# An XCiT attention and FFN kernel on one core: two transposes put together, loads reordered, one product for a whole and a left tile

## The chip, the cores and the metric

One core of a Trainium2 chip runs the whole kernel. The metric is the device time of one execution in microseconds (us). Executions are compared by their medians and by a ratio with a 95% interval.

## The reference

```python
def _attn_ref(q, k, v, tau):                      # q, k, v: 4 x 5824 x 256, fp32
    qn = q / (norm(q, axis=1) + 1e-06)            # norms run over the 5824 tokens
    kn = k / (norm(k, axis=1) + 1e-06)
    s = kn.transpose(0, 2, 1) @ qn / tau          # 256 x 256 scores for each batch
    a = np.exp(s - s.max(-1, keepdims=True))
    a /= a.sum(-1, keepdims=True) + 1e-09
    return v @ a

def _moe_ref(x, w1, w2, w3, w_out):               # x: 23296 x 256; w1, w2: 256 x 1024
    h = (x @ w1) * (x @ w2) @ w3                  # w3: 1024 x 1024
    return h @ w_out                              # w_out: 1024 x 256; out: 23296 x 256, fp32
```
(`norm` is written short for numpy's norm with its axis kept.)

## The kernel before

The kernel never forms `v @ a`. For each batch it folds the softmax matrix into w1 and w2 (eight "folds" into `Wf`), and it folds w3 and w_out into one matrix `W_sb` (eight "W units", once). What is left for each token is: two projections a and b of the transposed v by `Wf`, the product a*b, and one product with `W_sb`. A batch has eleven chunks of 512 tokens and a last chunk of 192: a "whole" tile of 128 tokens and 64 "left" ones. The left tokens of two batches are put together into one tile of 128, which is multiplied in the odd batch.

A step j of a chunk is four matmuls into PSUM banks of the tag "ab" (four banks), an ACT copy of a, a DVE product, and, two steps later (`LAG = 2`), the out matmuls into banks of the tag "out" (three banks):

```python
def emit_ab(b, c, j):
    ...                                    # 2 x 2 matmuls into tiles[0], tiles[1], tag "ab"
    nc.scalar.copy(a_sb[:, :n], tiles[0][:, :n])
    ...
    if n == 4 * P:
        nc.vector.tensor_mul(ab, a_sb, tiles[1])
    else:                                  # the 192-token chunk
        nc.vector.tensor_mul(ab[:, :P], a_sb[:, :P], tiles[1][:, :P])
        ...
        nc.vector.tensor_mul(lefts[b // 2][:, j, b % 2, :], a_sb[:, P:n], tiles[1][:, P:n])

def emit_out(b, c, j, ab):
    ...
    if small:
        lhs = [ab[:, :P]]
        if b % 2 == 1:
            lhs.append(lefts[b // 2][:, j, :, :].rearrange("p b t -> p (b t)"))
    ...
    for s, lhsT in enumerate(lhs):         # whole tile first, then the left tile
        ...
        nc.tensor.matmul(tl[h][:, o, :], lhsT=lhsT, rhs=W_sb[:, j, :], ...)
```

The sums of the softmax and the W units:

```python
def sum_mm(c2):
    ...
    if c2 == CT - 1:
        nc.vector.tensor_scalar_add(rs, m[:, :CT], 1e-9)
        nc.vector.reciprocal(rs, rs)

def w_unit(jt):
    m = psum.tile([P, 512], F32, tag="ab", name=f"w_{jt}", bufs=4)
    for lt in range(FT):
        nc.tensor.matmul(m[:, :D], lhsT=w3T[jt // 2][:, jt % 2, lt, :], rhs=wout_sb[:, lt, :], ...)
```

Everything else is put in order by an agenda: a list of works with the time, on a modelled clock, at which each is put into the program. While the chunks of a batch run, the agenda loads the pieces of v, q and k for later (through POOL's queue), transposes v by DMA, and in between computes scores, norms, exponentials and folds of the next batch. The load that follows a v piece is kept back by a "hold", a tiny POOL copy that reads what the transpose of that piece wrote, so that POOL's queue stands until the transpose is done.

```python
moves = [("qk", 1, 0, 29.0), ("v", 0, 3, 30.0), ("qk", 1, 1, 43.0), ("qk", 1, 2, 47.0), ("v", 0, 4, 53.0)]
moves += [("qk", 1, 3, 62.0), ("qk", 1, 4, 66.0), ("v", 0, 5, 72.0), ("qk", 1, 5, 81.0)]
moves += [("v", 1, 0, 94.0), ("v", 1, 1, 104.0), ("v", 1, 2, 114.0), ("qk", 2, 0, 126.0)]
t0, t1 = 54.0, 113.0
...
    if before is not None:
        at(t, 0.0, lambda w=before: hold(...))
...
soft = soft_units(n)                       # norms, k row, q norm, scores, exponentials, sums, folds
for i, (cst, t, fn) in enumerate(soft):
    at(t1 + 1.0 + t + (2.0 if b == 0 and i > 0 else 0.0), cst, fn)
```

## Time and profile before

| | before |
|---|---|
| device time, median of 3 runs | 572.44 us (572.33 to 573.01) |
| span of the profiled execution | 570.48 us |
| first projection starts | 37.59 us |
| first W unit starts, last W matmul starts | 64.61, 75.20 us |
| last matmul starts | 566.54 us |

How to read what follows. In a timeline a line gives the start in us, the length in us, the engine, the line of the kernel, the operation, what it writes and reads, and in brackets how long the engine had stood idle and what released it. In the table of waits a line gives the waiting instruction, what released it, the total us, the number of times and the longest. In the groups the columns are: busy us and mean ns of one, then the idle time before them.

TensorE's waits in the kernel before (the end of the table, without those for the first loads):

```profile
PE sum L328 <- ACT e L318: 0.8, 1, 0.8
PE a L463 <- DVE Wf L387: 0.6, 1, 0.6
PE w L627 <- ACT as L469: 0.2, 1, 0.2
PE a L463 <- ACT as L469: 0.2, 1, 0.2
PE fold L350 <- ACT as L469: 0.2, 1, 0.2
PE b L463 <- ACT Wf L357: 0.2, 1, 0.2
```

Each occurs once and none is over 0.8 us. The last three all fall between 168 and 182 us, where batch 0 goes over into batch 1.

The groups of DVE that the change touches (split by shape):

```profile
L480 DVE TENSOR_TENSOR abs<-as,b 128x128 bf16<-128x128 bf16 x32 | 9.1, 285 | 5.1 <-ACT as L469 2.9 <-PE o L504 0.7
L483 DVE TENSOR_TENSOR left<-as,b 128x64 bf16<-128x64 bf16 x32 | 6.9, 215 | 0.0
...
L334 DVE TENSOR_SCALAR rs<-sum 128x2 f32<-128x2 f32 x4 | 0.6, 153 | 0.4 <-PE sum L328 0.4
```

The two products of the 192-token chunks are 32 pairs; one addition of 1e-9 for each batch.

### The profile page before, as it was taken

To read this page: it belongs to the slowest core of one execution; us is meant where nothing else is said; L and a number is where in the kernel's file an instruction comes from. 1 tells how busy PE (TensorE), PEld (TensorE's weight loads), DVE (VectorE), ACT (ScalarE), POOL (GpSimd) and SP (SyncE) were. 2 spreads that over 40 slices of the span, in tenths; PEclk is the share of its full clock that TensorE was granted. 3 is DMA by queue.
4 is the path that set the end of the run, shared out by engine and by line. 5 is a ranking of instruction groups with operands and counts; after the bars stand their busy time and mean duration, and the time that the engine had idled before them with its cause. 6 is when DMAs were issued, how large, how long until landed. Compare 5 with 4: busy or idle time off the path is not lost.

```text
span 570.5 us, 10131 instructions
## 1 busy us (share of the span) xinstructions
PE 558.5 (98%) x3753; PEld 354.8 (62%) x3753; DVE 377.7 (66%) x613; ACT 339.9 (60%) x627; POOL 77.5 (14%) x164
## 2 busy tenths in 40 slices
PE   7889999999999999999999999999999999999997
PEld 4764576776656666666666666666665666666565
DVE  1047645788967577888766667787867656565564
ACT  1047535777765577777665567777766554454454
POOL 4260012212030110120210011020120000000000
PEclk9999999999999999999999999999999999999999
DMA  9999979897673696585761595756740325221011
GB/s 212 211 179 209 165 148 217 199 200 187 150 169 89 115 211 148 105 166 145 148 148 59 109 210 126 156 117 123 183 112 38 84 74 148 63 63 75 38 69 61
DMA packets 75104, 77.45 MB, mean 136 GB/s; under 512 B 54192, under 2 KB 58800, under 8 KB 75056
## 3 DMA queue, kind: packets, MB, share of 16 engines
q0 software_dynamic: 15760, 38.93, 39.3%
q1 hardware_dynamic: 59072, 37.69, 21.7%
q8 instruction: 29, 0.48, 0.3%
q10 hardware_dynamic: 224, 0.20, 0.1%
q14 instruction: 19, 0.16, 0.1%
HBM read 78.91 MB, written 23.86 MB: 180 GB/s over the span
## 4 chain that ended last, share of the span: by engine, by line
PE 91%; DMA 6%; ACT 1%; DVE 1%; issue 0%; POOL 0%; ACTq 0%; POOLq 0%
PE o L504 27%; PE a L463 27%; PE b L463 27%; PE G L188 5%; DMA k<-in_k_dram 5%; PE fold L350 2%; DMA w3T<-w_wout 1%; PE w L627 1%; ACT as L469 1%; PE quarter L376 0%; ACT kr L279 0%; POOL k L109 0%; DVE s L313 0%; ACT e L318 0%; DVE abs L478 0%
## 5 line engine op out<-in xcount | busy, mean ns | idle before, releaser
L478 DVE TENSOR_TENSOR abs<-as,b 128x512 bf16<-128x512 bf16 x336 | 230.3, 687 | 139.9 <-ACT as L469 127.3
L469 ACT CAST as<-a 128x512 bf16<-128x512 f32 (+1 forms) x384 | 215.9, 563 | 173.0 <-DVE abs L478 85.0
L463 PEld LDWEIGHTS <-Wf 128*128 128x128 bf16 x1536 | 149.0, 98 | 102.8 <-issue 2.3
L463 PE MATMUL a<-vT,Wf 128*128 128x512 bf16 x704 | 209.4, 379 | 0.8 <-DVE Wf L387 0.6
L504 PE MATMUL o<-W_sb,abs 128*128 128x256 bf16 x1376 | 209.9, 273 | 0.1
L463 PE MATMUL b<-vT,Wf 128*128 128x512 bf16 x704 | 209.4, 379 | 0.0
L504 PEld LDWEIGHTS <-abs 128*128 128x128 bf16 x1376 | 134.5, 98 | 81.9 <-DVE abs L480 0.3
L197 DVE TENSOR_TENSOR acc<-acc,sq 128x1024 f32<-128x1024 f32 x66 | 80.4, 1219 | 0.4 <-ACT sq L185 0.4
L188 PE MATMUL G<-k,q 128*128 128x256 bf16 x276 | 49.6, 273 | 0.0
L185 ACT ACTIVATE sq<-q 128x512 f32<-128x512 bf16 x66 | 41.8, 634 | 0.0
L185 ACT ACTIVATE sq<-k 128x512 f32<-128x512 bf16 x66 | 41.5, 630 | 0.0
L451 POOL COPY gate_t<-abs 1x1 bf16<-1x1 bf16 x39 | 9.6, 246 | 171.8 <-DVE abs L478 171.0
L525 DVE COPY osb<-o 128x512 f32<-128x512 f32 x44 | 30.1, 685 | 0.8 <-PE o L504 0.7
L188 PEld LDWEIGHTS <-q 128*128 128x128 bf16 x276 | 27.0, 98 | 3.1
L524 ACT COPY osb<-o 128x512 f32<-128x512 f32 x44 | 25.8, 586 | 3.8 <-PE o L504 1.8
L455 POOL COPY gate_t<-vT 1x1 bf16<-1x1 bf16 x17 | 3.6, 209 | 177.7 <-DMA vT<-v 177.7
L109 POOL DMA_DIRECT2D q<-in_q_dram x28 | 15.1, 539 | 13.0 <-DMA k<-in_k_dram 5.4
L279 ACT ACTIVATE kr<-row 128x256 f32<-128x256 f32 x1 | 0.4, 384 | 25.8 <-PE row L267 25.8
L357 ACT ACTIVATE Wf<-fold,rs 128x512 bf16<-128x512 f32 x15 | 10.3, 688 | 8.9 <-PE fold L350 7.7
L350 PE MATMUL fold<-w,e 128*128 128x512 bf16 x56 | 15.0, 379 | 0.2 <-ACT as L469 0.2
L478 DVE TENSOR_TENSOR abq<-as,b 128x512 bf16<-128x512 bf16 x16 | 10.8, 687 | 5.2 <-ACT as L469 4.6
L109 POOL DMA_DIRECT2D k<-in_k_dram x24 | 13.6, 566 | 4.1 <-DMA k<-in_k_dram 3.3
(95 smaller groups left out, 234.3 us busy)
## 6 DMA issues: line engine op xcount, KB each, us to landing
out_dram<-osb SPq DMA_DIRECT2D x44, 512.0 KB, 3.1
k<-in_k_dram POOLq DMA_DIRECT2D x19, 512.0 KB, 8.6
v<-in_v_dram POOLq DMA_DIRECT2D x19, 512.0 KB, 5.4
q<-in_q_dram POOLq DMA_DIRECT2D x18, 512.0 KB, 5.9
w_wout<-in_moe_w_dram POOLq DMA_DIRECT2D x1, 2048.0 KB, 23.5
k<-in_k_dram POOLq DMA_DIRECT2D x4, 320.0 KB, 6.6
v<-in_v_dram POOLq DMA_DIRECT2D x4, 320.0 KB, 5.0
q<-in_q_dram POOLq DMA_DIRECT2D x3, 320.0 KB, 4.3
```

Of the source, the lines that this page charges most:

```text
L109: nc.gpsimd.dma_start(out=pieces[nm, n, pi][:, lo:hi, :], in_=qk_main[nm, n][0][:, pi * PIECE + lo : pi * PIECE + hi, :])
L185: nc.scalar.activation(out=dst[:, :, part, :], in_=src[:, o : o + 2, :], func=AF.Square)
L188: nc.tensor.matmul(G[:, ct, :], lhsT=qt[:, i, ct * P : (ct + 1) * P], rhs=kt[:, i, :], start=(pr == 0 and part == 0 and ct == 0), stop=(pr ...
L197: nc.vector.tensor_add(accs[n], accs[n], sqs[0])
L350: nc.tensor.matmul(m, lhsT=st["e"][:, c2, c1 * P : (c1 + 1) * P], rhs=w12[:, c2, w, lo:hi], start=(c2 == 0), stop=(c2 == CT - 1),)
L357: nc.scalar.activation(out=dst, in_=m, func=AF.Copy, scale=st["rs"][:, c1 : c1 + 1])
L463: nc.tensor.matmul(t[:, :n], lhsT=Wf[b][:, ct, w, j * P : (j + 1) * P], rhs=rhs_of(b, c, ct), start=(ct == 0), stop=(ct == CT - 1),)
L469: nc.scalar.copy(a_sb[:, :n], tiles[0][:, :n])
L478: nc.vector.tensor_mul(ab, a_sb, tiles[1])
L504: nc.tensor.matmul(tl[h][:, o, :], lhsT=lhsT, rhs=W_sb[:, j, :], start=(j == 0 and o == 0), stop=(j == FT - 1 and (small or o == 1)), skip ...
L524: nc.scalar.copy(o[:, 0:2, :], tl[0])
L525: nc.vector.tensor_copy(o[:, 2:4, :], tl[1])
```

## The change

It has five parts. (1) In batch 0 the 1e-9 is put into the sums' bank by a tiny matmul ahead of them, so that the addition on DVE goes. (2) The W units take "out" banks in place of "ab" banks. (3) Batch 0's fourth and fifth v piece are loaded one behind the other and transposed together, without the hold between them, and the later loads move, so that none stands in POOL's queue before the norms' reduction; the 2.0 that pushed back the rest of the softmax go. (4) In the 192-token chunks one DVE product writes whole and left tile (for this the odd batches keep the left tokens ahead of the whole tile), and the left tile is multiplied first. (5) In the last chunk five steps are left pending in place of two.

```diff
+LAG_END = 5
+    tiny = consts.tile([1, P], F32)
+    nc.vector.memset(tiny, 1e-9)
...
+        def sum_start():
+            ...
+            if n == 0:
+                nc.tensor.matmul(
+                    st["sum"][:, :CT], lhsT=tiny, rhs=ones_pp[:1, :CT], start=True, stop=False, skip_group_check=True
+                )
...
-                    start=(c1 == 0 and c2 == 0), ...
+                    start=(n > 0 and c1 == 0 and c2 == 0), ...
...
-                nc.vector.tensor_scalar_add(rs, m[:, :CT], 1e-9)
-                nc.vector.reciprocal(rs, rs)
+                if n > 0:
+                    nc.vector.tensor_scalar_add(rs, m[:, :CT], 1e-9)
+                nc.vector.reciprocal(rs, rs if n > 0 else m[:, :CT])
...
+        if c == NCH - 1:
+            if b % 2 == 0 and j == 0:
+                lefts[b // 2] = work.tile([P, FT, 2, P + LEFT], BF16, tag="left", name=f"left_{b}", bufs=1)
+            both = lefts[b // 2][:, j, b % 2, :]
+            nc.vector.tensor_mul(both, a_sb[:, :n], tiles[1][:, :n])
+            ab = both[:, :P] if b % 2 == 0 else both[:, LEFT:]
...
-            nc.vector.tensor_mul(ab[:, :P], a_sb[:, :P], tiles[1][:, :P])
-            ...
-            nc.vector.tensor_mul(lefts[b // 2][:, j, b % 2, :], a_sb[:, P:n], tiles[1][:, P:n])
...
-        for s, lhsT in enumerate(lhs):
+        for s, lhsT in reversed(list(enumerate(lhs))) if small else enumerate(lhs):
...
-        m = psum.tile([P, 512], F32, tag="ab", name=f"w_{jt}", bufs=4)
+        m = psum.tile([P, 512], F32, tag="out", name=f"w_{jt}", bufs=3)
...
-            moves = [("qk", 1, 0, 29.0), ("v", 0, 3, 30.0), ("qk", 1, 1, 43.0), ("qk", 1, 2, 47.0), ("v", 0, 4, 53.0)]
-            moves += [("qk", 1, 3, 62.0), ("qk", 1, 4, 66.0), ("v", 0, 5, 72.0), ("qk", 1, 5, 81.0)]
-            moves += [("v", 1, 0, 94.0), ("v", 1, 1, 104.0), ("v", 1, 2, 114.0), ("qk", 2, 0, 126.0)]
+            moves = [("qk", 1, 0, 29.0), ("v", 0, 3, 30.0), ("v", 0, 4, 30.5), ("qk", 1, 1, 44.0), ("qk", 1, 2, 45.0)]
+            moves += [("qk", 1, 3, 53.0), ("qk", 1, 4, 55.0), ("v", 0, 5, 61.0), ("qk", 1, 5, 73.0)]
+            moves += [("v", 1, 0, 88.0), ("v", 1, 1, 98.0), ("v", 1, 2, 120.0), ("qk", 2, 0, 130.0)]
...
-            if before is not None:
+            if before is not None and not (nm == "v" and before == (m, pi - 1) == (0, 3)):
...
-            at(t1 + 1.0 + t + (2.0 if b == 0 and i > 0 else 0.0), cst, fn)
+            at(t1 + 1.0 + t, cst, fn)
...
+                lag = LAG_END if b == B - 1 and c == NCH - 1 else LAG
-                while w_ready[0] and len(pend) > LAG and npop < 2:
+                while w_ready[0] and len(pend) > lag and npop < 2:
```

More of the change, by code (lines that the diff above doesn't have):

```diff
@@ L158, in transpose_piece @@
             nc.sync.dma_start_transpose(vT[:, pi * PIECE : pi * PIECE + g, :, :], t[:, :g, :])
-            nc.sync.dma_start_transpose(vTt[:, :, :P], t[:, g, :])
-            nc.sync.dma_start_transpose(vTt[:, :, P:], t[:LEFT, g + 1, :])
+            first = n % 2 == 0
+            nc.sync.dma_start_transpose(vTt[:, :, :P] if first else vTt[:, :, LEFT:], t[:, g, :])
+            nc.sync.dma_start_transpose(vTt[:, :, P:] if first else vTt[:, :, :LEFT], t[:LEFT, g + 1, :])
     G_tiles = {}
@@ L320, in exps @@
             )
+        def sum_start():
+            st["sum"] = psum.tile([P, 512], F32, tag="out" if n == 0 else "G", name=f"sum_{n}", bufs=3 if n == 0 else 1)
+            Wf[n] = wf_pool.tile([P, CT, 2, F], BF16, tag="Wf", name=f"Wf_{n}")
+            if n == 0:
+                nc.tensor.matmul(
+                    st["sum"][:, :CT], lhsT=tiny, rhs=ones_pp[:1, :CT], start=True, stop=False, skip_group_check=True
+                )
         def sum_mm(c2):
-            if c2 == 0:
-                st["sum"] = psum.tile([P, 512], F32, tag="out" if n == 0 else "G", name=f"sum_{n}", bufs=3 if n == 0 else 1)
-                Wf[n] = wf_pool.tile([P, CT, 2, F], BF16, tag="Wf", name=f"Wf_{n}")
+            if c2 == 0 and n > 0:
+                sum_start()
             m = st["sum"]
@@ L329, in sum_mm @@
                     m[:, c1 : c1 + 1], lhsT=st["e"][:, c2, c1 * P : (c1 + 1) * P], rhs=ones_b,
-                    start=(c1 == 0 and c2 == 0), stop=(c1 == CT - 1 and c2 == CT - 1), skip_group_check=True,
+                    start=(n > 0 and c1 == 0 and c2 == 0), stop=(c1 == CT - 1 and c2 == CT - 1), skip_group_check=True,
                 )
@@ L402, in soft_units @@
         if n == 0:
-            return [k_first, k_row, q_first, scaled_first, first_folds, second_quarter] + [lambda i=i: fold(i) for i in range(4, 8)]
+            return [k_first, k_row, q_first, scaled_first, first_folds, second_quarter, sum_start] + [lambda i=i: fold(i) for i in range(4, 8)]
         return (
@@ L469, in emit_ab @@
         nc.scalar.copy(a_sb[:, :n], tiles[0][:, :n])
-        if b == 0 and c < 2:
-            if j % 4 == 0:
-                held[0] = in_pool.tile([P, 4, 512], BF16, tag="q", name=f"abq_{c}_{j}", bufs=IN_BUFS["q"])
-            ab = held[0][:, j % 4, :]
-        else:
-            ab = work.tile([P, 512], BF16, tag="ab_sb", name=f"abs_{b}_{c}_{j}", bufs=8 * NDEF + 6)
-        if n == 4 * P:
-            nc.vector.tensor_mul(ab, a_sb, tiles[1])
-        else:
-            nc.vector.tensor_mul(ab[:, :P], a_sb[:, :P], tiles[1][:, :P])
-            if b % 2 == 0 and j == 0:
-                lefts[b // 2] = work.tile([P, FT, 2, LEFT], BF16, tag="left", name=f"left_{b}", bufs=1)
-            nc.vector.tensor_mul(lefts[b // 2][:, j, b % 2, :], a_sb[:, P:n], tiles[1][:, P:n])
+        if c == NCH - 1:
[4 more added lines that the diff above has]
+            ab = both[:, :P] if b % 2 == 0 else both[:, LEFT:]
+        else:
+            if b == 0 and c < 2:
+                if j % 4 == 0:
+                    held[0] = in_pool.tile([P, 4, 512], BF16, tag="q", name=f"abq_{c}_{j}", bufs=IN_BUFS["q"])
+                ab = held[0][:, j % 4, :]
+            else:
+                ab = work.tile([P, 512], BF16, tag="ab_sb", name=f"abs_{b}_{c}_{j}", bufs=8 * NDEF + 2)
+            nc.vector.tensor_mul(ab, a_sb, tiles[1])
         pend.append((b, c, j, ab))
@@ L492, in emit_out @@
             if b % 2 == 1:
-                lhs.append(lefts[b // 2][:, j, :, :].rearrange("p b t -> p (b t)"))
+                lhs.append(lefts[b // 2][:, j, :, :].rearrange("p b t -> p (b t)")[:, P : P + 2 * LEFT])
         else:
@@ L618 @@
     soft0[3]()
+    soft0[6]()
     busy(3)
@@ L650, in make_agenda @@
             for i in range(4):
-                at((1.7, 2.6, 3.5, 3.9)[i], 0.43, soft0[6 + i])
+                at((1.7, 2.6, 3.5, 3.9)[i], 0.43, soft0[7 + i])
             at(0.0, 0.0, load_library)
@@ L689, in make_agenda @@
         soft = soft_units(n)
-        for i, (cst, t, fn) in enumerate(soft):
-            at(t1 + 1.0 + t + (2.0 if b == 0 and i > 0 else 0.0), cst, fn)
+        for cst, t, fn in soft:
+            at(t1 + 1.0 + t, cst, fn)
         agenda.sort()
```

## The prediction

> **What bounds the kernel now.** I read the page's busy table first, then the chain that ended last, then the timeline of TensorE in a steady stretch, and last the few places where TensorE stood still.
>
> ```profile
> PE 558.5 (98%) x3753; PEld 354.8 (62%) x3753; DVE 377.7 (66%) x613; ACT 339.9 (60%) x627; POOL 77.5 (14%) x164
> ...
> PE 91%; DMA 6%; ACT 1%; DVE 1%; issue 0%; POOL 0%; ACTq 0%; POOLq 0%
> ```
>
> TensorE is busy 98% of the span and is 91% of the chain; DMA's 6% of the chain is the load of q and k before 31 us. Busy is not yet proof of peak, so I take the steady stretch of the last batch:
>
> ```profile
> 550.39 0.59 PE L463 MATMUL a<-vT,Wf 128*128 128x512 bf16 x2
> 550.82 0.59 PE L463 MATMUL b<-vT,Wf 128*128 128x512 bf16 x2
> ...
> 551.25 0.60 PE L504 MATMUL o<-W_sb,abs 128*128 128x256 bf16 x4
> ...
> 551.69 0.59 PE L463 MATMUL a<-vT,Wf 128*128 128x512 bf16 x2
> ```
>
> One step (4 matmuls of 512 columns, 4 of 256: 3072 columns) takes 551.69 - 550.39 = 1.30 us; 3072 columns at 2.4 per ns are 1.28 us and 8 fixed parts of 2.5 ns are 0.02. There is no hole. So I went through all 3753 matmuls: the start of the next minus the start of this one, less columns/2400 + 0.0025 us. What is left over is lost time. It sums to 14.2 us of 565: 9.2 before 36 us (loads), 1.0 from 36 to 62, 0.65 from 62 to 76, 0.0 from 76 to 168, **1.69 from 168 to 185** (batch 0 goes over into batch 1), 0.1 from 185 to 300, 0.24 to 400, 0.35 from 424 to 445, 0.34 from 445 to 500 (nearly all in batch 2's 192-column chunk), **0.60 after 560**. After the last matmul there are 3.7 us of copies and output writes. No more than about 5 us after the first 36 can be won by better ordering, under 1% of 572.
>
> **What the Trainium skill says.** "TensorE: Matmul & The Clock Gate", section "Back-to-back issue gap", gives N/2.4 + 2.5 ns for a warm array; the step above agrees to 0.01 us (1.30 against 1.30), with a granted clock of 1.00 in every stretch. "Perfetto Trace Analysis", section "Identifying the Most-Contended Engine", warns that matmul busy share is no measure of headroom; hence the sum of leftovers above rather than the 98%. "PSUM — Partial Sum Buffer", section "The four PSUM rules", says that a starting matmul clears the marks of its bank and that later matmuls without the start flag add where a mark is set: so a first product of 1e-9 by 1 may stand in for the addition of 1e-9. No run before shows that; it is a matter of correctness, not time. "VectorE: DVE Perf Modes", section on the TRN2 errata, says that every instruction carries a fixed cost; the trace agrees: the product of 512 columns takes 687 ns, of 128 columns 285, of 64 columns 215, so about 1.05 ns a column and some 150 ns fixed.
>
> **The change part by part.**
>
> **1e-9 in the sum (batch 0).** It removes one DVE addition of 153 ns between the sums and the reciprocal, and adds one tiny matmul well before, where TensorE later sits idle 0.94 us anyway. The first projections may start up to 0.1 us sooner (the last quarter product ends at about the same time as the reciprocal). But all that is gained before 68 us is given back at the W units, which wait for transposed w3:
>
> ```profile
> 62.53 5.76 DMA w3T<-w_wout
> 68.34 1.92 PE w L627 x16
> ```
>
> The second of the four transposes lands at 62.53 + 5.76 = 68.29 and TensorE starts at 68.34, 0.24 us late. Its time comes from the load queue, which the change doesn't touch. Worth 0.0.
>
> **W units in out banks.** The first unit starts at 64.61, 0.38 us late, and the page puts 0.22 of it down to an ACT copy freeing an ab bank; but that copy ended at 64.58 and the first w3 transpose landed at 64.56 too. Taking away the bank wait leaves the transfer's. Worth 0.0, at most 0.1.
>
> **Fourth and fifth v piece together, loads earlier, POOL clear for the norms.** This is the part with money in it, indirectly. Before:
>
> ```profile
> 157.88 0.53 POOL L109 DMA_DIRECT2D v<-in_v_dram  x1 [0.40 <-issue]
> 158.44 3.19 POOL L258 PARTITION_ALL_REDUCE tot<-acc  x1
> ...
> 169.70 0.51 ACT L318 ACTIVATE e<-s,r 128x256 bf16<-128x256 f32 x1 [1.09 <-DVE s L313]
> ...
> 170.73 0.59 PE L463 MATMUL a<-vT,Wf 128*128 128x512 bf16 x2 [0.18 <-ACT as L469]
> ...
> 180.43 0.69 ACT L357 ACTIVATE Wf<-fold,rs 128x512 bf16<-128x512 f32 x1 [0.68 <-PE fold L350]
> ...
> 181.16 0.33 PE L463 MATMUL b<-vTt,Wf 128*128 128x192 bf16 x2 [0.17 <-ACT Wf L357]
> ```
>
> The reduction over partitions could have started at 154.7 (DVE's sum of the accumulators ends there) but stood in POOL's queue behind a load that waited for a transpose until 157. It ended at 161.63; ACT's k row followed at 161.66, and everything to the exponentials came late: 0.35 us lost on TensorE at 170.3. Then six of the eight folds fall among the 192-column products, whose four banks they share: 0.25 + 0.34 + 0.34 us lost at 178.7, 179.4 and 180.8, and small ones. In the change that load is scheduled after the norms, and the 2.0 us that pushed back the rest of the softmax are gone. The built order shows what follows: the sums stand two steps (2.6 us) earlier, six folds come before the first 192-column product and two just after; then no folds, and no scaled score between the last chunks. I expect 1.69 to become about 0.3: **-1.4 us** (0.9 to 1.7).
>
> The price is at 75 to 103 us. The fifth v piece is loaded right behind the fourth (+512 KB at some 2.4 us a piece, from landings at 79.85, 82.29, 84.72) and its transpose (3.6 us to landing) precedes the hold that frees the next q and k piece: free at about 91.2 in place of 88.5. The k piece that was issued at 89.57 landed at 98.25 and was needed at 102.67, so 4.4 us of room shrink to about 1.7. The later pieces gain: they no longer wait for the fifth piece's transpose (hold until 110.45). I expect no stall, -0.0.
>
> **One product for left and whole tile.** 32 pairs of 285 + 215 = 500 ns become one of about 0.15 + 192 x 1.05 = 355 ns: 4.6 us of DVE, nearly all beside other work. It pays only in the even batches' last chunk, where a step of TensorE is 4 x 82.5 + 109 = 439 ns, less than the 500 ns of DVE. Batch 2 loses 0.34 there; I expect **-0.25**. (Batch 0's share is in the 1.4.)
>
> **Left first, lag 5 at the end.** In an odd batch the left tile's bank is the one whose copy is still running (0.18 us lost at 311.5 and 562.65). Taking it first moves the whole tile's 0.11 us behind this wait: +0.1 in batch 1, made up by the shorter product. At the end:
>
> ```profile
> 566.06 0.29 DVE L480 TENSOR_TENSOR abs<-as,b 128x128 bf16<-128x128 bf16 x1
> ...
> 566.40 0.10 PEld L504 LDWEIGHTS <-abs 128*128 128x128 bf16 x1 [0.32 <-DVE abs L480]
> ...
> 566.86 0.42 DVE L519 COPY oleft<-o 128x256 f32<-128x256 f32 x1 [0.38 <-PE o L504]
> ```
>
> With five pending, 5 x 2 x 0.109 = 1.09 us of work lies behind the last product, so the 0.3 us wait goes. But four ab steps of 0.33 us then follow each other through four banks, with an ACT copy (0.32) and a DVE product (0.36) each, which costs some 0.3; and the whole tile's output, now last, is 0.11 us later for ACT. Sum: **0.0 +/- 0.3**.
>
> **Sum.** -1.4 - 0.25 + 0.1 - 0.1 + 0.0 = -1.65, taken back to -1.5 for small new waits: 572.44 - 1.5 = **570.9 us**, 0.3% faster.
>
> **The rivals.** (1) *A load comes late*: the k piece's room of 1.7 us is an estimate from one trace; if the fifth piece's transpose lands 2 us later than I think, TensorE stalls at about 102 us and the gain is halved: 571.5 to 572.5. For it: DMA share is 0.9 to 1.2 from 65 to 100 us. Against: later pieces have 3 to 9 us of room and all move earlier. (2) *The first third is looser than I say*: if the transposed w3 land earlier when POOL and banks are less crowded, 0.5 us more is won, 570.3. Against: their source is landed at 60.4 by a queue filled at 37 us. (3) *The tail turns*: five pending steps press on the four ab banks and the osb copies of the last full chunk delay the left tile's bank; +0.4 us, 571.3. (4) *DVE is the bound*, so that its 4.6 us count: against it 66% busy and no steady hole on TensorE.
>
> **Range and chances.** Gains between 0.6 and 2.4 us and a run spread of about 0.3 give 570.0 to 571.9. More than 2% is 11.4 us; all lost time after 36 us is 5 us, so faster by that is out, and slower needs a stall of 11 us, which only a wrongly ordered load could make.
>
> **What would show it.** After: TensorE's lost time from 168 to 185 falls to about 0.3; the reduction starts at about 155, straight after DVE's sum; no wait of the 192-column products for fold copies; DVE busy falls by some 4.7 us; the W units still start at 64.6 and 68.3; no G product waits for a k or q piece at 102. I am wrong if TensorE waits for a transfer between 100 and 150, or if the last matmul ends more than 0.5 us away from where the saved waits put it.

## The result and the profile after

| | before | after |
|---|---|---|
| device time, median of 6 runs each | 572.27 us (571.83 to 573.01) | 570.95 us (570.49 to 571.50) |
| ratio, 95% interval | | 0.9976 (0.9963 to 0.9989) |
| span of the profiled execution | 570.48 us | 569.46 us |

The result is correct. That does not show that the 1e-9 arrives: the scores are products of unit vectors, so each sum of 256 exponentials is over 90, where neighbouring fp32 numbers lie some 8e-6 apart. The changed kernel is 0.24% faster, and the interval lies below 1.

The page after: busy time, the chain by engine, and the group that took the place of the two products.

```profile
PE 558.9 (98%) x3755; PEld 354.9 (62%) x3755; DVE 375.7 (66%) x581; ACT 340.5 (60%) x627; POOL 77.2 (14%) x163
...
PE 91%; DMA 6%; ACT 1%; DVE 1%; POOL 0%; issue 0%; ACTq 0%; POOLq 0%
...
L488 DVE TENSOR_TENSOR left<-as,b 128x192 bf16<-128x192 bf16 x32 | 11.2, 353 | 5.7 <-ACT as L483 3.5
```

The bound is the same: TensorE, 91% of the chain. The groups of products fell by 9.1 + 6.9 - 11.2 = 4.8 us, but DVE as a whole by only 2.0 us, a difference that the fourth experiment explains.

TensorE's waits after, the same end of the table:

```profile
PE a L477 <- ACT Wf L399: 0.4, 1, 0.4
PE sum L341 <- ACT e L323: 0.4, 1, 0.4
PE w L643 <- DMA w3T<-w_wout: 0.3, 1, 0.3
```

The three waits of the transition are gone from the table, and the W units' wait now bears the name of the transfer. To put sizes to it I used the sum of leftovers of the prediction (start of the next matmul minus start of this one, less columns/2400 + 0.0025 us), by stage. Where a stage has a start in both traces, the difference of those starts gives the same result.

| lost TensorE time, us | before | after |
|---|---|---|
| before the first projection | 9.95 | 9.61 |
| up to the first W unit | 0.63 | 0.63 |
| W units | 0.26 | 0.47 |
| batch 0's last full chunk and 192-token chunk | 0.49 + 1.20 | 0.09 + 0.74 |
| batch 1's 192-token chunk | 0.24 | 0.18 |
| batch 2's 192-token chunk | 0.34 | 0.20 |
| batch 3's 192-token chunk | 0.60 | 0.61 |
| from the last matmul's start to the end of the span | 3.94 | 4.10 |

All other stretches are alike within 0.01 us. The start of the kernel gives 0.12 net (0.34 won before the first projection, 0.21 of it lost again at the W units), the transition 0.86, batches 1 and 2 together 0.20, and the end takes 0.17: 1.01 in sum, against 1.02 between the spans. The device times moved a little more, by 1.32 between the medians.

The transition's reading lines after, from the timeline:

```profile
154.70 3.24 POOL L263 PARTITION_ALL_REDUCE tot<-acc  x1 [10.85 <-DVE acc L261]
...
166.66 0.51 ACT L323 ACTIVATE e<-s,r 128x256 bf16<-128x256 f32 x1 [0.15 <-DVE s L318]
...
177.73 0.60 ACT L539 COPY osb<-o 128x512 f32<-128x512 f32 x1
...
178.15 0.68 DVE L540 COPY osb<-o 128x512 f32<-128x512 f32 x1
...
178.75 0.74 DVE L373 TENSOR_SCALAR Wf<-fold,rs 128x512 bf16<-128x512 f32 x1
```

The reduction starts as soon as DVE has its sum, as predicted, and the second exponential waits 0.15 us where it waited 1.09. But two folds still stand in the 192-token chunk. The fold's copy (0.74 us on DVE) comes right behind the output copies of the chunk before (0.60 on ACT, 0.68 on DVE), DVE starts no product from 178.15 to 179.41, and TensorE loses 0.13, 0.17 and 0.26 us at 178.5, 178.8 and 179.2.

The W units and the tail after:

```profile
64.27 0.77 PEld L643 LDWEIGHTS <-w3T 128*128 128x128 bf16 x8 [0.62 <-DMA w3T<-w_wout]
...
68.21 1.92 PE L643 MATMUL w<-w_wout,w3T 128*128 128x256 bf16 x16 [0.29 <-DMA w3T<-w_wout]
...
565.66 0.37 ACT L529 COPY osb<-o 128x256 f32<-128x256 f32 x1 [1.16 <-PE o L519]
...
566.52 0.53 ACTq L537 DMA_DIRECT2D out_dram<-oleft  x1
```

The first and the third W unit start with the landing of a transposed part of w3 (landed at 64.23 and 68.16 us, used from 64.27 and 68.21). In the tail, ACT's copy of the whole tile, now last, starts 0.30 us after the last matmul's start at 565.36, and the last output is issued 1.16 us after it.

### The profile page after: what moved, and what is told of

It is laid out like the page before. It is cut to its first block, busy times and chain, and to the rows that moved or that the text cites. A ratio compares the mean times of both kernels' runs of the same rounds, so it can differ in the third digit from the quotient of the medians.

```text
span 569.5 us, 10098 instructions
## 1 busy us (share of the span) xinstructions
PE 558.9 (98%) x3755; PEld 354.9 (62%) x3755; DVE 375.7 (66%) x581; ACT 340.5 (60%) x627; POOL 77.2 (14%) x163
## 4 chain that ended last, share of the span: by engine, by line
PE 91%; DMA 6%; ACT 1%; DVE 1%; POOL 0%; issue 0%; ACTq 0%; POOLq 0%
PE o L519 28%; PE b L477 27%; PE a L477 27%; PE G L193 5%; DMA k<-in_k_dram 5%; PE fold L364 2%; DMA w3T<-w_wout 1%; PE w L643 1%; ACT kr L284 0%; ACT as L483 0%; PE quarter L390 0%; POOL k L112 0%; DVE s L318 0%; ACT e L323 0%; DVE abs L498 0%
## 5 line engine op out<-in xcount | busy, mean ns | idle before, releaser
L519 PE MATMUL o<-W_sb,abs 128*128 128x256 bf16 x1344 | 201.1, 273 | 0.0
L519 PEld LDWEIGHTS <-abs 128*128 128x128 bf16 x1344 | 131.4, 98 | 80.8
L488 DVE TENSOR_TENSOR left<-as,b 128x192 bf16<-128x192 bf16 x32 | 11.2, 353 | 5.7 <-ACT as L483 3.5
```

Source lines behind the costliest of these rows:

```text
L488: nc.vector.tensor_mul(both, a_sb[:, :n], tiles[1][:, :n])
```

## The experiments

Twelve kernels were run, all with a correct result. The numbers, for comparison in one place: "last W" is the start of the last W matmul, "middle" runs from there to the start of the last matmul of all, "tail" from there to the end of the span. The middle holds the four batches except batch 0's first projections, and not the loads at the start, whose landings differ from run to run. The ratio is against runs of the kernel before on the same chip; their medians were 572.12 us beside e1 to e4, 571.86 beside e5, e7, e8 and e9, 571.74 beside e6 and e10, and 571.93 beside e11 and e12.

| kernel | last W | middle | tail | span | median of runs | ratio (95%) |
|---|---|---|---|---|---|---|
| before | 75.20 | 491.33 | 3.94 | 570.48 | 572.27 | |
| after | 75.08 | 490.28 | 4.10 | 569.46 | 570.95 | 0.9976 (0.9963 to 0.9989) |
| e1_schedule | 74.81 | 490.58 | 3.93 | 569.32 | 571.34 | 0.9980 (0.9950 to 1.0010) |
| e2_shift_only | 75.70 | 492.11 | 3.92 | 571.73 | 573.61 | 1.0020 (0.9994 to 1.0045) |
| e3_loads_only | 75.33 | 491.35 | 3.92 | 570.60 | 571.95 | 0.9993 (0.9967 to 1.0019) |
| e4_two_products | 74.61 | 490.66 | 4.08 | 569.35 | 571.46 | 0.9983 (0.9957 to 1.0009) |
| e5_lag2 | 75.29 | 490.22 | 4.08 | 569.60 | 571.26 | 0.9986 (0.9971 to 1.0001) |
| e6_lag2_whole_first | 74.85 | 490.22 | 3.92 | 569.00 | 570.46 | 0.9978 (0.9964 to 0.9993) |
| e7_w3_early | 75.07 | 490.28 | 4.10 | 569.45 | 570.89 | 0.9981 (0.9964 to 0.9998) |
| e8_w3_early_ab | 74.23 | 490.27 | 4.08 | 568.59 | 570.49 | 0.9979 (0.9964 to 0.9994) |
| e9_delay | 74.72 | 490.28 | 4.09 | 569.09 | 570.80 | 0.9982 (0.9967 to 0.9997) |
| e10_folds_early | 75.11 | 489.73 | 4.12 | 568.96 | 570.00 | 0.9965 (0.9949 to 0.9982) |
| e11_all | 74.06 | 489.66 | 3.93 | 567.65 | 569.59 | 0.9956 (0.9944 to 0.9969) |
| e12_all_lag2 | 74.25 | 489.68 | 3.96 | 567.89 | 569.71 | 0.9957 (0.9943 to 0.9971) |

Runs whose intervals overlap this much aren't told apart by their times; the places in the trace do that. Where "middle" agrees to 0.01 us over kernels that do not differ there (490.28, 490.28, 490.27, 490.28 for after, e7, e8 and e9), it shows how little chance enters it.

### e1: the schedule alone

The theory: the reordered loads and the earlier softmax (part 3) make nearly all of the gain. The rival: the single product (part 4) makes it.

```diff
 # the kernel before, with part 3 of the change only:
-            moves = [...]
+            moves = [("qk", 1, 0, 29.0), ("v", 0, 3, 30.0), ("v", 0, 4, 30.5), ...]
-            if before is not None:
+            if before is not None and not (nm == "v" and before == (m, pi - 1) == (0, 3)):
-            at(t1 + 1.0 + t + (2.0 if b == 0 and i > 0 else 0.0), cst, fn)
+            at(t1 + 1.0 + t, cst, fn)
```

> The kernel before with the schedule alone: new load times, fourth and fifth v piece together, batch 0's softmax 2.0 us earlier; two DVE products, W units in ab banks, lag 2 as before. Theory (the schedule carries the gain in the change of batches): reduction starts at 154.7 in place of 158.4, no 0.35 us wait at the scaled scores, lost TensorE time between the first 512-column product of the last full chunk and batch 1 falls from 1.69 to 0.8-1.0; the device time about 0.8 us below before. Rival (the one DVE product frees the 192-column products): the 192-column chunk still loses 1.2 or more, the gain under 0.4 us.

Measured: the middle shrank by 0.75 us (491.33 to 490.58), of the 1.05 that the whole change gives there. From the last W matmul to the start of batch 1 it is 107.10 before, 106.34 in e1 and 106.24 after. So the schedule is the larger part, 0.76 of 0.86 in the transition. The lost time of the 192-token chunk of batch 0 is 0.84, hardly more than with the whole change (0.74), so what is left there isn't the pair of products.

### e2 and e3: the two halves of the schedule

The schedule has two halves: the loads (the reduction runs early) and the softmax 2.0 earlier on the agenda. The prediction said that the late reduction was what made everything up to the exponentials late and cost 0.35 us at 170.3. If so, the loads alone (e3) remove that wait.

```diff
 # e2: the kernel before, and
-            at(t1 + 1.0 + t + (2.0 if b == 0 and i > 0 else 0.0), cst, fn)
+            at(t1 + 1.0 + t, cst, fn)
 # e3: the kernel before, with the new moves and the hold left out, and the 2.0 kept
```

> The kernel before with only the 2.0 us shift of batch 0's softmax taken away; load order as before, so the reduction still stands behind the held v load. Theory (POOL's queue is the cause): the reduction still starts at about 158.4 and ends at 161.6, ACT and DVE now wait for it by up to 2 us more, TensorE loses more at about 161 to 170 than before, total equal to before or up to 1.5 us slower. Rival (the 2.0 us alone were the cost): lost time in the change of batches falls to about 0.9, 0.8 us faster than before.

> The kernel before with only the new load order; the 2.0 us shift stays. Theory: the reduction starts at 154.7, the 0.35 us wait goes, but the folds stay where they were, so the 192-column chunk still loses 1.0 to 1.2 of TensorE's time: 0.3 us faster than before. Rival (an early reduction is enough): lost time falls to 0.8, as in the whole change.

Measured: e2 is 0.78 us slower in the middle, e3 is the same as before (491.35 against 491.33). From the timeline of e2 (the softmax earlier, the loads not moved):

```profile
158.80 3.19 POOL L258 PARTITION_ALL_REDUCE tot<-acc  x1
...
162.02 0.42 ACT L279 ACTIVATE kr<-tot 128x256 f32<-128x256 f32 x1 [2.92 <-POOL tot L258]
...
162.96 0.59 PE L463 MATMUL a<-vT,Wf 128*128 128x512 bf16 x2 [1.02 <-ACT as L469]
```

ACT stands 2.92 us for the late reduction with the copies of a behind it, and TensorE loses 1.18 us there and 0.35 in the step after. From the timeline of e3 (the loads moved, the softmax not earlier):

```profile
155.00 3.24 POOL L258 PARTITION_ALL_REDUCE tot<-acc  x1 [12.31 <-DVE acc L256]
...
169.82 0.51 ACT L318 ACTIVATE e<-s,r 128x256 bf16<-128x256 f32 x1 [1.09 <-DVE s L313]
...
170.85 0.59 PE L463 MATMUL a<-vT,Wf 128*128 128x512 bf16 x2 [0.19 <-ACT as L469]
```

The reduction starts at 155.00 and is done at 158.24, more than 8 us before the first score, and still the exponential waits 1.09 us and TensorE 0.35 in all. So the prediction's cause for this wait has fallen. What makes it is the order in which the two engines have their works: ACT's exponential waits for DVE's score, which stands behind DVE's product, which waits for ACT's copy of a (1.09 us on ACT, then 1.05 on DVE in the kernel before), and this twice in a row. Put 2.0 earlier on the agenda, the same works meet the chunk's steps at another place (the first exponential at 165.52 finds its score done, the second waits 0.15), and the wait is gone. The early reduction gives nothing by itself (e3). It is what allows the earlier order, and e2 shows the price of that order without it. That the meeting place of these works makes the wait is read from the timelines; what the runs show is that the 2.0 earlier takes it away once the reduction is early (e1 against e3).

### e4: two products again

The theory: the single product gives about 0.25 in batch 2, and a small part of the transition. The rival: DVE's time counts throughout.

```diff
 # the kernel after, and
-            nc.vector.tensor_mul(both, a_sb[:, :n], tiles[1][:, :n])
+            nc.vector.tensor_mul(both[:, wl], a_sb[:, wl], tiles[1][:, wl])    # wl, ll: columns of whole and left tile
+            nc.vector.tensor_mul(both[:, ll], a_sb[:, ll], tiles[1][:, ll])
```

> The changed kernel with the one 192-column DVE product taken apart again into 128 and 64 columns. Theory: batch 2's last chunk loses 0.34 again in place of 0.20, batch 0's last chunk loses 0.1 to 0.4 more than 0.74, the tail up to 0.3 more; together 0.3 to 0.8 us slower than the change. Rival (DVE hidden anyway): no lost time on TensorE moves by more than 0.1.

Measured: the middle is 0.38 us longer than after. By places, 0.10 of it are in batch 0, 0.06 in batch 1, 0.15 in batch 2 and 0.06 in batch 3's end. DVE's busy time is 377.4 us, as before (377.7), against 375.7.

Why do 32 pairs at 500 ns cost so little more than 32 products at 353? DVE's timeline of the kernel before, in batch 2's 192-token chunk:

```profile
444.01 0.29 DVE L480 TENSOR_TENSOR abs<-as,b 128x128 bf16<-128x128 bf16 x1
444.22 0.21 DVE L483 TENSOR_TENSOR left<-as,b 128x64 bf16<-128x64 bf16 x1
444.35 0.68 DVE L525 COPY osb<-o 128x512 f32<-128x512 f32 x1
```

The second product starts 0.21 us after the first, while the first's record lasts 0.29: the records overlap. Over the 32 pairs the median from the first's start to the second's end is 0.42 us, not 0.50. So one product in place of two saves 0.42 - 0.353 = 0.066 us, and 32 x 0.066 = 2.1 us; DVE's busy time fell by 2.0 with the whole change, and by 1.7 from e4 to after. And 0.42 is less than the 0.439 us of a step of TensorE, so the pair kept pace with TensorE by itself; where the next pair follows with no wait it even starts 0.33 us after the first (444.95 and 445.28 in the same chunk). As I read it, the loss comes from the output copy (0.68) between the products, which still stands there after the change, and the shorter product only makes it up sooner; no run moves the output copies. The Trainium skill agrees: "Perfetto Trace Analysis", section "Per-instruction lifecycle: what the profiler-reported window actually captures", says that a DVE record ends with the acknowledgement of the write and that the next instruction may begin before that.

### e5 and e6: the pending steps and the left tile first

The theory: lag 5 and lag 2 cost the same at the end, one wait exchanged for another; and left first makes the last output later. The rival: lag 5 takes away the 0.3 us of waiting at the end.

```diff
 # e5: the kernel after, and
-LAG_END = 5
+LAG_END = 2
 # e6: e5, and
-        for s, lhsT in reversed(list(enumerate(lhs))) if small else enumerate(lhs):
+        for s, lhsT in enumerate(lhs):
```

> The changed kernel with the lag at the end back at 2; left still first. Theory (the five pending steps exchange one wait for another): the tail's lost time stays at 0.6 +/- 0.15, the wait of about 0.3 before the last products comes back, the two waits of 0.19 on the ab banks go. Rival (the lag is worth its 0.3): lost time after the last chunk's start rises to 0.9.

> The changed kernel with the end as before: lag 2 and the whole tile first; the one DVE product stays. Theory (left first costs after the last matmul, the lag gives nothing): last matmul at the same distance from the W units as in the change within 0.1 us; from the start of the last matmul to the end of the span 3.93 us in place of 4.10; 0.1 to 0.2 us faster than the change. Rival (the end of the change is a gain): last matmul 0.3 us later, no less time after it.

Measured: with lag 2 the middle is 0.06 shorter (490.22 in both) than with lag 5. Batch 3's last chunk loses 0.55 against 0.61: with lag 5 there are two waits of 0.19, by their times for "ab" banks (the first ends 0.05 us after the product that frees its bank), which lag 2 exchanges for one of 0.32 at the last products. The order of the tiles shows in the tail, 3.92 with the whole tile first and 4.08 with the left one first. The timeline of e6:

```profile
564.95 0.39 PE L519 MATMUL o<-W_sb,left 128*128 128x256 bf16 x2 [0.16 <-DVE left L488]
...
565.27 0.37 ACT L529 COPY osb<-o 128x256 f32<-128x256 f32 x1 [0.77 <-PE o L519]
...
566.10 0.54 ACTq L537 DMA_DIRECT2D out_dram<-oleft  x1
```

ACT's copy of the whole tile starts 0.20 us after the start of the last matmul (565.07 in this run), where it was 0.30 after; the last output is issued 1.03 us after that start, where it was 1.16. Over all fourteen profiles, the seven with the whole tile first have a tail of 3.92 to 3.96 and the seven with the left one first 4.08 to 4.12, whatever the lag. In batch 1 left first does no harm: its 192-token chunk takes 5.00 us in after, e5 and e6 alike.

### e7, e8 and e9: what the W units wait for

The W units were predicted to wait for the transposed w3, not for banks, and all gain before them to be given back. Three kernels test this: w3's load one piece earlier in its queue (e7), the same with the banks of the kernel before (e8), and 0.43 us of useless matmuls put ahead of the W units (e9). The rivals: banks are the wait (then e8 loses 0.2 to 0.4), or TensorE's own work is (then e9 is 0.43 slower there).

```diff
 # e7: the kernel after, and
-    load_piece("v", 0, 2)
     nc.gpsimd.dma_start(out=wout_sb, ...)
     nc.gpsimd.dma_start(out=w3_bf, in_=w3r)
+    load_piece("v", 0, 2)
 # e8: e7, and
-        m = psum.tile([P, 512], F32, tag="out", name=f"w_{jt}", bufs=3)
+        m = psum.tile([P, 512], F32, tag="ab", name=f"w_{jt}", bufs=4)
 # e9: the kernel after, and
+            at(15.0, 0.0, lambda: busy(2))         # two matmuls of 512 columns into an unused bank
             at(15.0, 0.0, transpose_w3)
```

> The changed kernel with w3 and w_out loaded before the third v piece. Theory (the W units wait for w3's transfer and nothing else): the w3 load lands about 2.4 us earlier, the lost 0.29 + 0.45 us at the W units go, and 0.7 us are won against the change; the third v piece lands at about 60 and its transpose is still done by 75, no new wait at the fifth chunk. Rival (another wait stands behind it): less than 0.3 won.

> As the run with w3 early, but W units in ab banks as in the kernel before. Theory (in the change the out banks bring nothing because the transfer hides it): with the transfer out of the way the ab bank's wait for the ACT copy shows, 0.2 to 0.4 us at each W unit that follows a product, 0.3 us or more lost in all. Rival (the banks never mattered): within 0.1 us of the run with out banks.

> The changed kernel with two idle 512-column matmuls (0.43 us of TensorE) put in before the W units. Theory (time won or lost before the W units is absorbed by the transfer of w3): the first W unit starts no more than 0.15 us later, the last W unit ends within 0.1 us of the change, the lost time at the W units falls from 0.74 to about 0.35; total within 0.1 of the change. Rival (the start is on the path): everything after is 0.43 us later.

Measured: e9's first W unit starts 27.06 us after the first projection, in after it is 27.02, and in both it starts 0.05 us after the first transpose has landed (64.33 and 64.23 us). The wait at this unit fell from 0.29 to 0.03 us; another 0.11 of the 0.43 us was made up before, where after waits for v's second piece and e9 doesn't. So the transfer sets this start, and the wait has room for 0.29 us and no more. From e9's timeline, the weight loads of the first two groups of W units:

```profile
64.38 0.77 PEld L643 LDWEIGHTS <-w3T 128*128 128x128 bf16 x8 [0.36 <-DMA w3T<-w_wout]
65.91 0.97 PEld L643 LDWEIGHTS <-w3T 128*128 128x128 bf16 x8
```

The next group, which waited until 68.21 after, found its half landed by 65.96 in this run, so that the last W matmul came 0.36 us earlier although there was more to do. The edit need not be the reason: the second of the four transposes lands at 65.9 to 66.9 us in four of the runs that leave its load alone and at 67.9 to 68.4 in six.

In e8, with w3 loaded early, the W units lost 0.00 in "ab" banks; the last W matmul started at 74.23, 0.85 earlier than after. So the banks did not matter here, and my own expectation for e8 missed. In e7 the W units' waits were gone as well, but its last W matmul was no earlier (75.07). TensorE's waits of e7 tell why:

```profile
PE tr_I-615_616 L135 <- DMA v<-in_v_dram: 0.8, 1, 0.8
```

v's second piece landed at 45.5 us in this run, and the transposes of it on TensorE waited 0.8 us. This happened in three of the twelve profiles of experiments, with or without the edit, so e7's missing gain has its cause in another load, which came late in this run.

### e10: the last two folds out of the 192-token chunk

The theory from the profile after: the two folds left in that chunk cost most of its 0.74 us, since their copies meet the output copies. The rival: the output copies alone do it.

```diff
 # the kernel after, and (n == 1 is prepared during batch 0)
-            + [(0.2, 16.5, sums)]
-            + [(0.43, 17.5 + 1.1 * i, lambda i=i: fold(i)) for i in range(8)]
+            + [(0.2, 16.5 - (1.3 if n == 1 else 0.0), sums)]
+            + [(0.43, 17.5 - (1.3 if n == 1 else 0.0) + 1.1 * i, lambda i=i: fold(i)) for i in range(8)]
```

> The changed kernel with batch 0's sums and folds 1.3 us earlier still, so that all eight folds stand before the first 192-column product. Theory (what is left there is folds' copies and the output copies of the last full chunk meeting in the 192-column chunk): the chunk's lost time falls from 0.74 to 0.25 or less, from the W units to the last matmul 490.28 becomes 489.8. Rival (the chunk is bound by ACT and DVE themselves): it stays above 0.5.

Measured: the loss in that chunk fell from 0.74 to 0.20 and the middle by 0.55 (490.28 to 489.73). The timeline of e10:

```profile
176.65 0.75 DVE L373 TENSOR_SCALAR Wf<-fold,rs 128x512 bf16<-128x512 f32 x1 [0.37 <-PE fold L364]
...
178.20 0.68 DVE L540 COPY osb<-o 128x512 f32<-128x512 f32 x1
...
178.80 1.14 DVE L488 TENSOR_TENSOR left<-as,b 128x192 bf16<-128x192 bf16 x3
```

The last fold's copy is over at 177.40, ahead of the output copy at 178.20, and DVE is back at the products at 178.80. So the two folds cost 0.54 us there. The 0.20 that stay I take for the output copies' own share, since batch 2, which has no fold in its chunk, loses the same 0.20; no run moves those copies. And e10 takes both the folds' copies and their "ab" banks out of the chunk: whether a fold would do harm there with a bank of its own, it does not show.

### e11 and e12: put together

Together: w3 early, the transposes of v's second piece 3 us later on the agenda (so that they don't wait when it lands late), the folds early, the whole tile first, and a lag of 3 (e11) or 2 (e12) at the end.

```diff
 # the kernel after with the edits of e7 and e10 and the whole tile first, and
-LAG_END = 5
+LAG_END = 3                                        # e12: 2
-            at(7.0, 0.5, lambda: transpose_half_on_pe(0, 1, 0, True))
-            at(8.0, 0.5, lambda: transpose_half_on_pe(0, 1, 1, False))
+            at(10.0, 0.5, lambda: transpose_half_on_pe(0, 1, 0, True))
+            at(11.0, 0.5, lambda: transpose_half_on_pe(0, 1, 1, False))
```

> The best version that the runs point to: the changed kernel with w3 and w_out loaded before the third v piece, the second v piece's transposes on TensorE 3 us later, batch 0's sums and folds 1.3 us earlier, the whole tile first, lag 3 at the end. Theory (the parts add up): W units end at 74.2 as in the run with w3 early and ab banks, from there to the last matmul 489.6 to 489.7, then 3.93 to the end: span 567.8, about 1.6 us below the change. Rival (w3 early collides with the third v piece or the later transposes): W units end at 75 and the span is at most 0.8 below the change.

> As the run before with lag 2 at the end. Theory: within 0.1 us of lag 3, since lag 2 leaves a wait of 0.3 before the last products and lag 3 one of about 0.2 on the ab banks. Rival (one more pending step is a gain): lag 3 ends 0.2 us or more earlier.

Measured: e11 took 569.59 us (569.42 to 569.81), e12 569.71 (569.50 to 569.72), where the kernel before took 571.93. The ratio to before is 0.9956 (0.9944 to 0.9969). All five times of e11 and of e12 lie below after's lowest (570.49). They were run at other times. In both profiles no wait for v's second piece and none at the W units is left. The piece landed at 43.9 and 44.5 us, though, early enough without the later transposes (e8: 44.1 and no wait), so these runs don't test that edit. The lag makes no difference that these runs show (0.02 in the middle, 0.03 in the tail).

## Why the prediction was right

The time was predicted as 570.9 us (570.0 to 571.9) and measured as 570.95, faster by less than 2%, as the chances had it. By its own steps:

- **The bound.** That only some 5 us were to be won after 36 us, and that a microsecond is won in few places, held: TensorE stayed at 98% and at 91% of the chain. One thing the prediction left out: the Trainium skill, "TensorE: Matmul & The Clock Gate", section "Back-to-back issue gap", gives N/2.4 + 2.5 ns for a single matmul, and some 131 ns for 512 columns in a steady stream; here a steady stream keeps to the formula (216 ns from start to start, median of all 512-column matmuls), so the sum of leftovers stands on the trace.
- **1e-9 in the sum: 0.0 predicted, -0.12 measured for the whole start.** The step from the first sum to the first projection is 1.71 us with the addition and 1.52 without it, in every profile where I measured it: 0.19, where at most 0.1 was expected. With earlier landings of loads 0.34 us were won up to the first projection and 0.21 of it was given back at the W units. That it is given back was right, up to the 0.29 us that e9 finds in the wait.
- **W units' banks: 0.0 predicted, 0.0 measured** (e8). Reading past the label of that wait, to the landing of the transfer, was right.
- **The loads' room.** The fifth v piece's place cost nothing, as predicted: the hold that frees the next pieces ran at 92.4 us (predicted 91.2), the k piece landed at 100.85 and was needed at 102.55, so the room was 1.7 us, the number that the prediction gives. No score product waits. The first rival did not come about. Two readings of the prediction were off here: the next k piece landed later and not earlier (108.11 in place of 104.40), without a wait, and the DMA share that it quotes was 1.02 and 0.89 from 65 to 75 and 75 to 100 us.
- **The transition: -1.4 predicted, -0.86 measured.** This is the term that was mis-sized. The prediction saw from the built order that two folds come "just after" the first 192-token product and took their cost for small (and of the kernel before it counted six folds in that chunk, where the trace has five); e10 sizes it at 0.54 (0.74 lost with them, 0.20 without; with the full chunk's 0.09 that leaves 0.29 in the transition, the 0.3 of the prediction). And its cause for one of the waits was wrong: the late reduction did not make the 0.35 us wait at 170.3 (e3 keeps the wait with an early reduction). By the timelines the wait came from the order of works on ACT and DVE. The step "everything to the exponentials came late" fails; that the gain comes from the schedule holds (e1: 0.76 of 0.86).
- **One product: -0.25 in batch 2 predicted, -0.14 to -0.15 measured.** The step that failed is "32 pairs of 285 + 215 = 500 ns". Records of successive DVE instructions overlap; a pair takes 0.42 us. So DVE wasn't slower than TensorE's 0.439, and DVE's busy time fell by 2.0 us and not by 4.7. The Trainium skill could have warned: "VectorE: DVE Perf Modes", section "The DRAIN you can't avoid", first says that the next operation does not start until the pipeline has emptied, but then that one that is not held starts earlier. The trace agrees: with no wait between them the second product started 0.204 us after the first (median of 32 pairs), 0.08 us before the first's record ended.
- **Left first and lag 5: 0.0 +/- 0.3 predicted, +0.01 before the last matmul and +0.16 behind it.** Within what was said, and of both sub-steps: the wait on four banks came (two of 0.19), and the whole tile's output, now last, came later. The +0.1 expected for batch 1 did not show (-0.06 with the shorter product).
- **The sum.** The parts gave -1.65, taken back to -1.5; the spans differ by 1.02 and the medians by 1.32. So by the traces the gain was put 0.5 us too high, and the medians moved 0.3 us more than the spans, which is within the spread of the runs (1.0 us from the lowest to the highest). That the time is met to 0.05 us is partly luck; that it lies within the range is not.
- **The rivals.** No load came late (rival 1), and DVE's time did not count beyond the 192-token chunks (rival 4). The start won 0.12 us of the 0.5 that rival 2 allows, and the tail cost 0.17 of the 0.4 of rival 3.
- **What would show it.** The reduction at 155: yes (154.70). The lost time in the transition at about 0.3: no, 0.83. No wait for fold copies in the 192-token chunk: no, TensorE's at 179.2 us ends with the fold copy of 178.75. DVE busy down by some 4.7: no, 2.0. W units at 64.6 and 68.3: yes but for the earlier start (64.3 and 68.2). No wait for a transfer between 100 and 150 us: yes. The last matmul within 0.5 us of where the saved waits put it: just (1.18 earlier, the parts said 1.65).

Still open: why the second transpose of w3 lands at either about 66 or about 68 us (the runs show both for the same program order, and nothing in these traces says what decides it), and what the output copies in the 192-token chunks cost by themselves.

## What to carry to other kernels

When one engine is the bound at 98%, sum up its leftovers place by place and change only what stands at those places. Ahead of the end of such a stage, the copies of the work before and of the work for the next stage meet on the same two engines: keep them a few steps apart, as the early folds did (0.54 us). Before you charge two short instructions of one engine with the sum of their records, look whether the second starts within the first; and before you blame a late input for a wait, look how long the input had been there, or move it alone.

## What the Trainium skill lacked or had wrong

- "VectorE: DVE Perf Modes", section on the TRN2 errata: its table, with a source in PSUM, gives (120 + 192)/0.96 = 325 ns for the product of 192 columns and 658 for 512. The records last 353 and 687, and where one such product follows another with no wait they start 272 and 605 apart (medians); the table's figure is neither. The section's formula for an addition in fp32, (N + 151)/0.96, gives 357 and 691, and 291 and 224 for 128 and 64 columns (records of 285 and 215): this is the one to use for the records of such products.
- "DMA: Bandwidth & Descriptors", section "Latency and other measured facts", gives a rate for transposes (261 GB/s, or 350 to 400) but for a transpose no time to landing and no spread. Here transposes of 512 KB from SBUF to SBUF landed 3.6 to 6.6 us after their issue, and the second of w3's four landed at about 66 or about 68 us in runs of the same order; 2 us is more than this whole change is worth.
- "Perfetto Trace Analysis", section "Per-instruction lifecycle: what the profiler-reported window actually captures", does not say that records can be missing. In ten of these fourteen traces 7 or 8 of some 3755 matmuls are missing (busy table: x3745 to x3749; before and after have all of theirs), and each leaves what looks like a hole of 0.22 us on TensorE.
- No page has the time of the all-reduce over partitions on POOL that this kernel uses: 3.19 to 3.24 us for 128x512 in fp32. (The page on GpSimd has one for another instruction, `tensor_reduce` along the partitions.)
